# Slot tiles of a top-1 expert layer: rows turned by DMA transposes, the expert's middle feature-major, the gate at the output, three tiles in a runtime branch

## The chip, the cores and the metric

The kernel runs on one core of a Trainium2 chip. The time is the device time of one execution in microseconds; the time given for a kernel is the median over its runs. A profiled execution has a time of its own, and the span of its trace lies inside that time.

## The reference

Attention over 8 batches, 12 heads, 448 positions and head size 64, with queries and keys normalised by their root mean square, gives a matrix x of 3584 tokens by 768 features. On it follows a feed-forward layer with a dense part and eight experts, of which each token takes one:

```python
h_dense = np.maximum(x @ w1_dense, 0.0)
y_dense = h_dense @ w2_dense
logits = x @ w_gate
expert_idx = np.argmax(logits, axis=1)
...
gate_w = probs[np.arange(N), expert_idx]
for e in range(E):
    mask = expert_idx == e
    h = np.maximum(x[mask] @ w1[e], 0.0)
    y_moe[mask] = gate_w[mask, None] * (h @ w2[e])
return (y_dense + y_moe).astype(np.float32)
```

Here w1 and w1_dense are 768 by 512, w2 and w2_dense 512 by 768. The inputs are the same random draw each time.

## The kernel before

The kernel has two stages. In the first, `period(g)` walks through the attention, two heads at a time per step, and along with it computes for finished batches the expert choice, the gate and the dense part's hidden layer `relu(x @ w1_dense)`. For each token it writes one record of 704 words to a table in DRAM, `rec`: 768 bf16 values of x, 512 bf16 values of the dense hidden layer, the gate as a float, and padding. All expert weights are loaded into one SBUF tile `we` during this stage.

The second stage begins at line 528. Tokens are sorted by expert into slots; 128 slots make a slot tile, and each slot tile belongs to one expert, so that an expert's last tile may be partly empty. For 3584 tokens and eight experts there are at most NTL = 3584/128 + 7 = 35 tiles, and the kernel runs all 35, whether they hold tokens or not: an empty slot reads the record of row 0 and has an output row out of bounds, which is not written. Lines 534 to 597 compute on VectorE, from the counts of each expert, the row of each slot (`row`), its output row (`dest`) and the expert of each tile (`tei`, int32).

For each tile t the steps are:

- `gather(t)`: an indirect DMA on the POOL queue brings 128 records to `xg`.
- `xtrans(t)`: ten TensorE transposes turn the x values (six blocks of 128 columns) and the dense hidden values (four) into PSUM; VectorE copies them to `xT` and `hdT` (lines 614 and 619).
- `gemm1(t)`: TensorE loads the expert's number from `tei` into a register. Six matmuls, with a block of `xT` as the stationary operand and 512 columns of the expert's first weight as the moving one, give 128 tokens by 512 hidden features. ScalarE applies relu and, as the scale, the gate (line 630).
- `htrans(t)`: four TensorE transposes turn this hidden tile; ScalarE copies it to `heT` (line 637).
- `gemm2(t)`: eight matmuls of 384 columns with the dense hidden values and eight with the expert's add up in one PSUM tile `yp`. VectorE copies one half to `ys`, then ScalarE the other (lines 655 and 656), and an indirect DMA on POOL scatters the rows to the output (line 657).

The order on TensorE and on POOL is written out by hand at the end (lines 666 to 684): after a start-up, iteration t issues `gather(t + 4)`, `gemm1(t + 1)`, `xtrans(t + 2)`, `gemm2(t)` and `htrans(t + 1)`. The last weight load is issued on POOL in iteration 0. VectorE and ScalarE are ordered by the framework. The SP queue has nothing to do in this stage. A matmul is issued as two instructions, a load of the stationary operand (PEld) and the multiplication with the moving one (PE). Where an operand lies in `we` at a place that depends on the expert's register, TensorE's sequencer computes the address with a register instruction ahead of it (FUSED_REGOPS in the trace).

Of the kernel before, what the change touches and what calls it, by code (L numbers as in the profile page):

```python
# [9 lines left out]
F32 = mybir.dt.float32  # L10
BF16 = mybir.dt.bfloat16
I32 = mybir.dt.int32
AF = mybir.ActivationFunctionType
ALU = mybir.AluOpType
# [4 lines left out]
def kernel(  # L19
# [14 lines left out]
    nc = tc.nc  # L34
    P = 128
    B, H, S, D = q.shape
    N = B * S
    Dm = H * D
    E = moe_w_gate.shape[1]
    F = moe_w1_dense.shape[1]  # L40
# [4 lines left out]
    KD = Dm // P  # L45
    FT = F // P
    HD = Dm // 2
    De = D + 1
    scale = 1.0 / (D ** 0.5)
    PE, DVE, ACT, POOL, SP = (mybir.EngineType.PE, mybir.EngineType.DVE,  # L50
                              mybir.EngineType.Activation, mybir.EngineType.Pool,
                              mybir.EngineType.SP)
# [5 lines left out]
    ident = const.tile([P, P], BF16)  # L58
# [13 lines left out]
    NTL = N // P + E - 1  # L72
# [3 lines left out]
    GO = XH + F // 2  # L76
    RC = GO + 64
# [18 lines left out]
    we = const.tile([P, E, 2, KD * F], BF16)  # L96
# [3 lines left out]
    def constants():  # L100
# [11 lines left out]
        for hh in range(2):  # L112
# [3 lines left out]
            for n in range(NC4):  # L116
# [7 lines left out]
    wjobs = [(wgb, moe_w_gate.rearrange("(ko p) e -> p ko e", p=P)),  # L124
             (wd1, moe_w1_dense.rearrange("(ko p) f -> p ko f", p=P)),
             (wd2, moe_w2_dense.rearrange("(fo p) d -> p fo d", p=P))]
# [6 lines left out]
    one = ctx.enter_context(tc.tile_pool(name="m_one", bufs=1))  # L133
    with tc.tile_pool(name="a_ld", bufs=2) as ld, \
# [3 lines left out]
        xin, sqs, ssqs, rs, xn, qkT, exs, xas, xTs, avs, trs, xps = [{} for _ in range(12)]  # L138
# [132 lines left out]
        def xtrans(g):  # L271
            b, gb = divmod(g, NPR // GP)
            if g + 4 >= NG:
                trs["x"] = wkp.tile([P, 1024], BF16, tag="wk", name="xt")
            ps = trs["x"][:, :GP * S].rearrange("p (i s) -> p i s", i=GP)
            for i in range(GP):
                for m in range(4):
                    nc.tensor.transpose(  # L278
                        ps[:, i, QC[m]:QC[m] + P],
                        xas[b][:, m, (gb * GP + i) * P:(gb * GP + i + 1) * P], ident)  # L280
            xps[g] = trs["x"][:, :GP * S]
# [102 lines left out]
        def period(g):  # L384
            b, gb = divmod(g, NB)
            more = g + 2 < NG, g + 3 < NG
            for i in range(J):
# [3 lines left out]
                if i == 0:  # L391
                    if g > 1:
                        xtrans(g - 2)
                    if more[0]:
                        normalise(g + 2, "k")
                        normalise(g + 2, "q")
                    if gb != 1:
                        fill(g, KD)
# [60 lines left out]
        def run(order):  # L459
            with tc.manual_schedule(engines=order):  # L460
# [43 lines left out]
                for g in range(NG):  # L504
                    period(g)

                xtrans(NG - 2)
                xturned(NG - 2)
                fill(NG, KD)
# [16 lines left out]
        run({PE, POOL, SP, DVE, ACT})  # L526

    with tc.tile_pool(name="m_sb", bufs=5) as sb, \
         tc.tile_pool(name="m_p1", bufs=3, space=bass.MemoryType.PSUM) as ps1, \
         tc.tile_pool(name="m_p2", bufs=2, space=bass.MemoryType.PSUM) as ps2, \  # L530
         tc.tile_pool(name="m_ph", bufs=1, space=bass.MemoryType.PSUM) as psh, \
         tc.tile_pool(name="m_py", bufs=1, space=bass.MemoryType.PSUM) as psy:

        cnt = counts[B % 2]
        cmp = one.tile([P, E, NM], F32, tag="w1")
# [6 lines left out]
        tsi = one.tile([P, E], F32)  # L542
# [13 lines left out]
        for c in (slice(0, NC4 // 2), slice(NC4 // 2, NC4)):  # L556
# [3 lines left out]
            for i in range(2):  # L560
                nc.vector.tensor_mul(val[:, i, :, c], tl[:, :, c],
                                     tok[:, i, c].unsqueeze(1).to_broadcast(shape))
        slp = ps2.tile([P, 2, NTL], F32, tag="he")
        for n in range(NC4):
            nc.tensor.matmul(slp, sel[:, n // 4, n % 4], val[:, :, :, n],
                             start=(n == 0), stop=(n == NC4 - 1))
        sl = one.tile([P, 2, NTL], F32)
        nc.vector.tensor_copy(sl, slp)
        t1 = one.tile([P, NTL], F32)
        nc.vector.scalar_tensor_tensor(t1, in0=sl[:, 0], scalar=float(D), in1=sl[:, 1],  # L570
                                       op0=ALU.mult, op1=ALU.add)
# [5 lines left out]
                                ts[:1].unsqueeze(1).to_broadcast([1, NTL, E]), ALU.is_ge)  # L577
        te = one.tile([1, NTL], F32)
        nc.vector.tensor_reduce(te, tcm, AX.X, ALU.add)
        tei = one.tile([1, NTL], I32)  # L580
        nc.vector.tensor_scalar(tei, te, 1.0, None, op0=ALU.subtract)

# [9 lines left out]
                                       op0=ALU.mult, op1=ALU.add)  # L592
        nc.vector.scalar_tensor_tensor(t2, in0=sl[:, 1], scalar=float(J), in1=t2,
                                       op0=ALU.mult, op1=ALU.add)
        dest = one.tile([P, NTL], I32)
        nc.vector.scalar_tensor_tensor(dest, in0=t2, scalar=float(S - J + 1), in1=emp,
                                       op0=ALU.subtract, op1=ALU.add)

        xgs, xTs, hdTs, hes, heTs, eregs, stores = {}, {}, {}, {}, {}, {}, []

        def gather(t):
            xg = sb.tile([P, RC], F32, tag="xg", name="xg")
            nc.gpsimd.indirect_dma_start(  # L603
                out=xg, out_offset=None, in_=rec,
                in_offset=bass.IndirectOffsetOnAxis(ap=row[:, t:t + 1], axis=0))
            xgs[t] = xg

        def xtrans(t):
            xb = xgs[t].bitcast(BF16)
            xp = ps1.tile([P, KD, P], BF16, tag="tr")  # L610
            for kk in range(KD):
                nc.tensor.transpose(xp[:, kk], xb[:, kk * P:(kk + 1) * P], ident)
            xTs[t] = sb.tile([P, KD, P], BF16, tag="xT", name="xT")
            nc.vector.tensor_copy(xTs[t], xp)  # L614
            hp = ps1.tile([P, FT, P], BF16, tag="tr")
            for i in range(FT):
                nc.tensor.transpose(hp[:, i], xb[:, Dm + i * P:Dm + (i + 1) * P], ident)
            hdTs[t] = sb.tile([P, FT, P], BF16, tag="hdT", name="hdT")
            nc.vector.tensor_copy(hdTs[t], hp)

        def gemm1(t):
            eregs[t] = nc.tensor.value_load(tei[:, t:t + 1], min_val=0, max_val=min(t, E - 1))
            he = ps2.tile([P, F], F32, tag="he")
            for kk in range(KD):
                nc.tensor.matmul(he, xTs[t][:, kk],  # L625
                                 we[:, bass.ds(eregs[t], 1), 0, kk * F:(kk + 1) * F]
                                 .rearrange("p o f -> p (o f)"),
                                 start=(kk == 0), stop=(kk == KD - 1))
            hes[t] = sb.tile([P, F], BF16, tag="hs", name="hs")
            nc.scalar.activation(hes[t], he, AF.Relu, scale=xgs[t][:, GO:GO + 1])  # L630

        def htrans(t):
            hp = psh.tile([P, FT, P], BF16, tag="hp")
            for i in range(FT):
                nc.tensor.transpose(hp[:, i], hes[t][:, i * P:(i + 1) * P], ident)  # L635
            heTs[t] = sb.tile([P, FT, P], BF16, tag="heT", name="heT")
            nc.scalar.copy(heTs[t], hp)  # L637

        def gemm2(t):

            yp = psy.tile([P, 2, 512], F32, tag="y")
            for i in range(FT):
                for dd in range(2):
                    nc.tensor.matmul(yp[:, dd, :HD], hdTs[t][:, i],  # L644
                                     wd2[:, i, dd * HD:(dd + 1) * HD],
                                     start=(i == 0), stop=False)
            for i in range(FT):
                for dd in range(2):
                    nc.tensor.matmul(yp[:, dd, :HD], heTs[t][:, i],  # L649
                                     we[:, bass.ds(eregs[t], 1), 1,  # L650
                                        i * Dm + dd * HD:i * Dm + (dd + 1) * HD]
                                     .rearrange("p o f -> p (o f)"),
                                     start=False, stop=(i == FT - 1))
            ys = sb.tile([P, 2, HD], F32, tag="ys")
            nc.vector.tensor_copy(ys[:, 0], yp[:, 0, :HD])  # L655
            nc.scalar.copy(ys[:, 1], yp[:, 1, :HD])  # L656
            i = nc.gpsimd.indirect_dma_start(  # L657
                out=out, out_offset=bass.IndirectOffsetOnAxis(ap=dest[:, t:t + 1], axis=0),
                in_=ys.rearrange("p a d -> p (a d)"), in_offset=None,
                bounds_check=N - 1, oob_is_err=False)  # L660

            for j in stores:
                tc.declare_no_dep(i.ins, j.ins, reason="each token has one slot")
            stores.append(i)

        with tc.manual_schedule(engines={PE, POOL}):
            for t in range(4):
                gather(t)
            for t in range(2):
                xtrans(t)  # L670
            gemm1(0)
            htrans(0)
            for t in range(NTL):
                if t + 4 < NTL:
                    gather(t + 4)
                if t == 0:
                    nc.gpsimd.dma_start(*wjobs[-1])
                if t + 1 < NTL:
                    gemm1(t + 1)
                if t + 2 < NTL:  # L680
                    xtrans(t + 2)
                gemm2(t)
                if t + 1 < NTL:
                    htrans(t + 1)


# [28 lines left out]
```

## Time and profile before

| | us |
|---|---|
| runs | 462.23, 461.86, 455.8 |
| median | 461.86 |
| profiled execution | 458.04 |
| span of its trace | 456.3 |

| engine | busy us | share of the span |
|---|---|---|
| PE (matmul) | 384.7 | 84% |
| PEld (weight load) | 239.3 | 52% |
| DVE | 255.7 | 56% |
| ACT | 238.8 | 52% |
| POOL | 240.6 | 53% |

The mean granted TensorE clock is 0.956. In the slot stage the first gather is issued at 277.24 us, the first matmul of `gemm1` starts at 284.01, and the last matmul of the kernel ends at 451.07.

Engines are PE (TensorE's matmuls), PEld (its weight loads), DVE (VectorE), ACT (ScalarE), POOL (GpSimd) and SP (SyncE); a name with q is the engine's sequencer or queue, so PEldq holds TensorE's register instructions. A row such as `L625 PE MATMUL he<-we,xT` stands for the instructions of line 625 that write tile `he` from `we` and `xT`. The page cuts the span into 40 slices and gives each engine's busy share in tenths; PEclk is the granted clock in tenths. Busy times of pipelined matmuls overlap, so that the distance between two starts says what a matmul costs in a stream, and its duration doesn't.

### The profile page before, as it was taken

How to read it: one execution, taken by the hardware profiler on the slowest of the kernel's cores; microseconds unless marked ns; L12 is line 12 of the kernel's file. 1: busy time of each engine (PE TensorE's matmuls, PEld its weight loads, DVE VectorE, ACT ScalarE, POOL GpSimd, SP SyncE). 2: the span in 40 equal slices, each digit the busy share in tenths (PEclk: the TensorE clock that was granted, in tenths of full speed). 3: DMA queues.
4: the chain of work that ended last, by engine and by line, in shares of the span. 5: the costliest groups of instructions: out<-in, count | busy, mean ns of one | idle time of the engine just before them, and what ended most of it. 6: DMA issues, size and time to landing. Idle time of an engine off the chain costs nothing.

```text
span 456.3 us, 13950 instructions
## 1 busy us (share of the span) xinstructions
PE 384.7 (84%) x5628; PEld 239.3 (52%) x5628; DVE 255.7 (56%) x744; ACT 238.8 (52%) x394; POOL 240.6 (53%) x275
## 2 busy tenths in 40 slices
PE   0557777988969889798897954899999999999994
PEld 0234554555645556455564633466666666666662
DVE  2565679788897888978875553233232333323230
ACT  2735677785876868768687210333242333334241
POOL 2385887596775877759651105134444353444422
PEclk9999989998998999989999995999999999999998
DMA  8579395977979689796669984553544545354420
GB/s 212 185 112 244 100 249 144 225 153 222 228 229 213 135 241 225 230 213 139 157 100 200 178 194 133 110 172 121 174 129 147 165 137 167 127 171 154 161 95 1
DMA packets 49759, 76.32 MB, mean 167 GB/s; under 512 B 8541, under 2 KB 45661, under 8 KB 49696
## 3 DMA queue, kind: packets, MB, share of 16 engines
q0 software_dynamic: 24544, 43.31, 43.7%
q1 hardware_dynamic: 24832, 32.12, 22.4%
q8 instruction: 46, 0.75, 0.7%
q14 instruction: 17, 0.14, 0.1%
q10 hardware_dynamic: 320, 0.00, 0.0%
HBM read 73.98 MB, written 23.86 MB: 214 GB/s over the span
## 4 chain that ended last, share of the span: by engine, by line
issue 32%; DVE 21%; PE 21%; POOL 16%; ACT 4%; DMA 4%; POOLq 1%; ACTq 0%; DVEq 0%
DVE ssq L192 8%; PE ff L365 8%; POOL xg L603 7%; PE av L259 5%; DVE xa L268 4%; PE sc L241 3%; PE xt L278 3%; POOL out_dram L657 3%; POOL sq L187 3%; DVE y L227 2%; DVE y L229 2%; DMA records<-hd 2%; ACT we L244 2%; DVE y L211 2%; DMA gk<-in_g_k_dram 2%
## 5 line engine op out<-in xcount | busy, mean ns | idle before, releaser
L244 ACT ACTIVATE we<-sc 128x896 bf16<-128x896 f32 x168 | 147.0, 917 | 46.3 <-PE sc L241 45.7
L657 POOL DMA_INDIRECT out_dram<-ys,dest x35 | 35.3, 1010 | 95.2 <-ACT ys L656 90.5
L241 PE MATMUL sc<-y 64*64 64x448 bf16 x672 | 69.9, 408 | 7.9 <-ACT we L244 5.2
L637 ACT COPY heT<-hp 128x512 bf16<-128x512 bf16 x35 | 20.5, 585 | 91.7 <-PE hp L635 91.7
L259 PE MATMUL av<-va,we 64*128 64x65 bf16 x2688 | 63.9, 198 | 4.4 <-issue 3.5
L259 PEld LDWEIGHTS <-we 64*128 64x128 bf16 x2688 | 51.4, 99 | 26.4 <-issue 23.2
L211 POOL TENSOR_TENSOR y<-xk,r 128x448 bf16<-128x448 f32 x46 | 42.1, 937 | 41.7 <-ACT r L205 41.7
L192 DVE TENSOR_REDUCE ssq<-sq 128x7 f32<-128x448 f32 x96 | 55.4, 611 | 12.0 <-POOL sq L187 7.9
L655 DVE COPY ys<-yp 128x384 f32<-128x384 f32 x35 | 19.5, 558 | 72.5 <-issue 55.7
L365 PE MATMUL ff<-wd,xT 128*128 128x512 bf16 x192 | 52.1, 413 | 8.3 <-DVE xa L268 5.6
L625 PE MATMUL he<-we,xT 128*128 (+1 forms) x210 | 52.3, 386 | 0.5 <-issue 0.5
L644 PE MATMUL yp<-wd,hdT 128*128 128x384 bf16 x280 | 51.2, 326 | 1.1 <-ACT ys L656 1.1
L649 PE MATMUL yp<-we,heT 128*128 (+1 forms) x280 | 51.2, 326 | 0.0
L603 POOL DMA_INDIRECT xg<-records,row x35 | 34.5, 986 | 30.4 <-DVE t L591 20.0
L187 POOL TENSOR_TENSOR sq<-xk 128x448 f32<-128x448 f32 x44 | 40.7, 938 | 16.8 <-DVE ssq L192 16.7
L614 DVE COPY xT<-xp 128x768 bf16<-128x768 bf16 x35 | 19.5, 558 | 51.0 <-PE he L625 35.0
L219 PE MATMUL tr<-ident,y 128*128 128x128 bf16 x336 | 26.9, 237 | 20.0 <-DVE y L211 15.0
L268 DVE TENSOR_TENSOR xa<-av,inv 128x256 bf16<-128x256 f32 x96 | 40.8, 425 | 3.3
L187 POOL TENSOR_TENSOR sq<-xq 128x448 f32<-128x448 f32 x44 | 40.1, 932 | 0.0
L630 ACT ACTIVATE hs<-he,xg 128x512 bf16<-128x512 f32 x35 | 24.0, 687 | 27.8 <-PE he L625 18.1
L241 PEld LDWEIGHTS <-y 64*64 64x64 bf16 x672 | 20.5, 107 | 32.9 <-issue 22.9
L649 PEld LDWEIGHTS <-heT 128*128 128x128 bf16 x280 | 27.4, 98 | 18.1
(105 smaller groups left out, 475.6 us busy)
## 6 DMA issues: line engine op xcount, KB each, us to landing
we<-in_moe_w_dram POOLq DMA_DIRECT2D x16, 768.0 KB
xq<-in_q_dram SPq DMA_DIRECT2D x24, 448.0 KB, 4.8
xk<-in_k_dram SPq DMA_DIRECT2D x24, 448.0 KB, 5.7
xv<-in_v_dram POOLq DMA_DIRECT2D x11, 448.0 KB
records<-xa SPq DMA_DIRECT2D x8, 576.0 KB, 9.2
records<-hd SPq DMA_DIRECT2D x24, 128.0 KB, 3.9
wd<-in_moe_w_dense_dram POOLq DMA_DIRECT2D x2, 768.0 KB
records<-xa SPq DMA_DIRECT2D x8, 96.0 KB, 9.0
```

What stands on the lines that cost most here:

```text
L187: nc.gpsimd.tensor_mul(sqs[name, g, hh], x, x)
L192: nc.vector.tensor_reduce(ssqs[g][:, "qk".index(name), hh], sqs[name, g, hh].rearrange("p (j d) -> p j d", d=D), AX.X, ALU.add)
L211: eng.tensor_mul(y[:, :, hh], xin[name, g][:, hh].rearrange("p (j d) -> p j d", d=D), rs[name, g][:, hh].unsqueeze(2).to_broadcast([P, J, D]))
L241: nc.tensor.matmul(ps[r * D:(r + 1) * D, hh, :S], kT[rows, r, j], qT[rows, r].rearrange("p j s -> p (j s)"), start=True, stop=True)
L244: nc.scalar.activation(x, ps[:, :, :S], AF.Exp, scale=scale)
L259: nc.tensor.matmul(avs[hh, r][:, m], exs[g, j][rows, hh, QC[m]:QC[m] + P], va[rows, hh, j, :De], start=(j == 0), stop=(j == J - 1))
L268: nc.vector.tensor_mul(xas[b][:, :, h * D:(h + 1) * D], avs[hh, r][:, :, :D], inv.to_broadcast([P, 4, D]))
L365: nc.tensor.matmul(ff[0], xTs[b][:, kk, QC[m]:QC[m] + P], wd1[:, kk], start=(kk == 0), stop=(kk == KD - 1))
L603: nc.gpsimd.indirect_dma_start(out=xg, out_offset=None, in_=rec, in_offset=bass.IndirectOffsetOnAxis(ap=row[:, t:t + 1], axis=0))
L625: nc.tensor.matmul(he, xTs[t][:, kk], we[:, bass.ds(eregs[t], 1), 0, kk * F:(kk + 1) * F] .rearrange("p o f -> p (o f)"), start=(kk == 0), ...
L644: nc.tensor.matmul(yp[:, dd, :HD], hdTs[t][:, i], wd2[:, i, dd * HD:(dd + 1) * HD], start=(i == 0), stop=False)
L649: nc.tensor.matmul(yp[:, dd, :HD], heTs[t][:, i], we[:, bass.ds(eregs[t], 1), 1, i * Dm + dd * HD:i * Dm + (dd + 1) * HD] .rearrange("p o ...
```

## The change

The slot stage is rewritten; the first stage and the computation of `row`, `dest` and `tei` stay.

- `xtrans` goes. In its place `turn(t)` issues one DMA transpose on the SP queue that turns all 1280 bf16 columns of `xg` into `xT` with ten blocks of 128.
- `gemm1` computes the hidden tile feature-major: the stationary operand is a 128 x 128 block of the expert's first weight, the moving one a block of `xT`, so that 24 matmuls of 128 columns take the place of six of 512, and `htrans` goes too. ScalarE applies relu alone.
- `gemm2` keeps its sixteen matmuls, but the dense and the expert's part go to two PSUM tiles. ScalarE copies the dense part to `ds`; VectorE multiplies the expert's part by the gate and adds `ds`.
- The loop becomes the function `slots(t0, t1)`. It runs for the first NT1 = 32 tiles; after them every engine loads the number of tiles in use (`tct`), and the last three run in a branch that is taken only if that number is over 32.
- Buffers: `xg` has seven in place of five; the PSUM pools are two banks for the hidden tile and three double banks for the outputs.

```diff
-        def xtrans(t):
-            xb = xgs[t].bitcast(BF16)
-            xp = ps1.tile([P, KD, P], BF16, tag="tr")
-            for kk in range(KD):
-                nc.tensor.transpose(xp[:, kk], xb[:, kk * P:(kk + 1) * P], ident)
...
+        def turn(t):
+
+            xTs[t] = sb.tile([P, KD + FT, P], BF16, tag="xT", name="xT")
+            nc.sync.dma_start_transpose(xTs[t], xgs[t].bitcast(BF16)[:, :2 * GO])
+
+        def gemm1(t):
+
+            eregs[t] = nc.tensor.value_load(tei[:, t:t + 1], min_val=0, max_val=min(t, E - 1))
+            he = psh.tile([P, FT, P], F32, tag="he")
             for i in range(FT):
...
+                for kk in range(KD):
+                    c = kk * F + i * P
+                    nc.tensor.matmul(he[:, i],
+                                     we[:, bass.ds(eregs[t], 1), 0, c:c + P]
+                                     .rearrange("p o f -> p (o f)"), xTs[t][:, kk],
+                                     start=(kk == 0), stop=(kk == KD - 1))
+            hTs[t] = sb.tile([P, FT, P], BF16, tag="hT", name="hT")
+            nc.scalar.activation(hTs[t], he, AF.Relu)
...
-            yp = psy.tile([P, 2, 512], F32, tag="y")
+            yd = psy.tile([P, 2, 512], F32, tag="y", name="yd")
             for i in range(FT):
                 for dd in range(2):
-                    nc.tensor.matmul(yp[:, dd, :HD], hdTs[t][:, i],
+                    nc.tensor.matmul(yd[:, dd, :HD], xTs[t][:, KD + i],
                                      wd2[:, i, dd * HD:(dd + 1) * HD],
-                                     start=(i == 0), stop=False)
+                                     start=(i == 0), stop=(i == FT - 1))
+            ds = sb.tile([P, 2, HD], F32, tag="ds")
+            nc.scalar.copy(ds, yd[:, :, :HD])
+            ye = psy.tile([P, 2, 512], F32, tag="y", name="ye")
...
-            nc.vector.tensor_copy(ys[:, 0], yp[:, 0, :HD])
-            nc.scalar.copy(ys[:, 1], yp[:, 1, :HD])
+            nc.vector.scalar_tensor_tensor(ys, in0=ye[:, :, :HD], scalar=xgs[t][:, GO:GO + 1],
+                                           in1=ds, op0=ALU.mult, op1=ALU.add)
...
+        def slots(t0, t1, weights=None):
+            ahead = 4
+            for t in range(t0, min(t0 + ahead, t1)):
                 gather(t)
+                turn(t)
+            gemm1(t0)
+            for t in range(t0, t1):
+                if t + ahead < t1:
+                    gather(t + ahead)
+                    turn(t + ahead)
+                if t == t0 and weights:
+                    nc.gpsimd.dma_start(*weights)
+                if t + 1 < t1:
+                    gemm1(t + 1)
                 gemm2(t)
...
+        NT1 = N // P + E // 2
+        with tc.manual_schedule(engines={PE, POOL, SP}):
+            slots(0, NT1, wjobs[-1])
+        used = nc.values_load(tct, min_val=1, max_val=NTL)
+        with tc.If(used > NT1):
+            with tc.manual_schedule(engines={PE, POOL, SP}):
+                slots(NT1, NTL)
```

More of the change, by code (lines that the diff above doesn't have):

```diff
@@ L528 @@
     with tc.tile_pool(name="m_sb", bufs=5) as sb, \
[L529 to L532, printed above, removed]
+         tc.tile_pool(name="m_ph", bufs=2, space=bass.MemoryType.PSUM) as psh, \
+         tc.tile_pool(name="m_py", bufs=3, space=bass.MemoryType.PSUM) as psy:
         cnt = counts[B % 2]
@@ L562 @@
                                      tok[:, i, c].unsqueeze(1).to_broadcast(shape))
-        slp = ps2.tile([P, 2, NTL], F32, tag="he")
+        slp = psh.tile([P, 2, NTL], F32, tag="he")
         for n in range(NC4):
@@ L579 @@
         nc.vector.tensor_reduce(te, tcm, AX.X, ALU.add)
+        tct = one.tile([1, 1], I32)
+        nc.vector.tensor_copy(tct, tsi[:1, E - 1:])
         tei = one.tile([1, NTL], I32)
@@ L597 @@
                                        op0=ALU.subtract, op1=ALU.add)
-        xgs, xTs, hdTs, hes, heTs, eregs, stores = {}, {}, {}, {}, {}, {}, []
+        xgs, gts, xTs, hTs, eregs, stores = {}, {}, {}, {}, {}, []
         def gather(t):
-            xg = sb.tile([P, RC], F32, tag="xg", name="xg")
+            xg = sb.tile([P, RC], F32, tag="xg", name="xg", bufs=7)
             nc.gpsimd.indirect_dma_start(
@@ L606, in gather @@
             xgs[t] = xg
-        def xtrans(t):
-            xb = xgs[t].bitcast(BF16)
-            xp = ps1.tile([P, KD, P], BF16, tag="tr")
-            for kk in range(KD):
[L612 to L619, printed above, removed]
+        def turn(t):
+            xTs[t] = sb.tile([P, KD + FT, P], BF16, tag="xT", name="xT")
+            nc.sync.dma_start_transpose(xTs[t], xgs[t].bitcast(BF16)[:, :2 * GO])
@@ L621, in gemm1 @@
         def gemm1(t):
             eregs[t] = nc.tensor.value_load(tei[:, t:t + 1], min_val=0, max_val=min(t, E - 1))
[L623 to L629, printed above, removed]
@@ L630, in gemm1 @@
-            nc.scalar.activation(hes[t], he, AF.Relu, scale=xgs[t][:, GO:GO + 1])
-        def htrans(t):
-            hp = psh.tile([P, FT, P], BF16, tag="hp")
-            for i in range(FT):
-                nc.tensor.transpose(hp[:, i], hes[t][:, i * P:(i + 1) * P], ident)
-            heTs[t] = sb.tile([P, FT, P], BF16, tag="heT", name="heT")
-            nc.scalar.copy(heTs[t], hp)
+            he = psh.tile([P, FT, P], F32, tag="he")
+            for i in range(FT):
+                for kk in range(KD):
[4 more added lines that the diff above has]
+                                     start=(kk == 0), stop=(kk == KD - 1))
@@ L647, in gemm2 @@
+            ds = sb.tile([P, 2, HD], F32, tag="ds")
+            nc.scalar.copy(ds, yd[:, :, :HD])
+            ye = psy.tile([P, 2, 512], F32, tag="y", name="ye")
             for i in range(FT):
                 for dd in range(2):
-                    nc.tensor.matmul(yp[:, dd, :HD], heTs[t][:, i],
+                    nc.tensor.matmul(ye[:, dd, :HD], hTs[t][:, i],
                                      we[:, bass.ds(eregs[t], 1), 1,
@@ L652, in gemm2 @@
                                      .rearrange("p o f -> p (o f)"),
-                                     start=False, stop=(i == FT - 1))
+                                     start=(i == 0), stop=(i == FT - 1))
             ys = sb.tile([P, 2, HD], F32, tag="ys")
-            nc.vector.tensor_copy(ys[:, 0], yp[:, 0, :HD])
-            nc.scalar.copy(ys[:, 1], yp[:, 1, :HD])
+            nc.vector.scalar_tensor_tensor(ys, in0=ye[:, :, :HD], scalar=xgs[t][:, GO:GO + 1],
+                                           in1=ds, op0=ALU.mult, op1=ALU.add)
             i = nc.gpsimd.indirect_dma_start(
@@ L664, in gemm2 @@
             stores.append(i)
-        with tc.manual_schedule(engines={PE, POOL}):
-            for t in range(4):
+        def slots(t0, t1, weights=None):
+            ahead = 4
+            for t in range(t0, min(t0 + ahead, t1)):
                 gather(t)
[L669 to L678, printed above, removed]
+                turn(t)
[7 more added lines that the diff above has]
+                if t + 1 < t1:
                     gemm1(t + 1)
-                if t + 2 < NTL:
-                    xtrans(t + 2)
                 gemm2(t)
-                if t + 1 < NTL:
-                    htrans(t + 1)
+        NT1 = N // P + E // 2
[5 more added lines that the diff above has]
+                slots(NT1, NTL)
 _INS = ['q', 'k', 'v', 'g_q', 'g_k', 'moe_w_gate', 'moe_w1_dense', 'moe_w2_dense', 'moe_w1', 'moe_w2']
```

## The prediction

> **What bounds the kernel now.** I read the page's slices first, then the busy time of each engine in the even part of the slot stage, the TensorE groups there, and last the starts of TensorE's own register instructions within one tile.
>
> ```profile
> PE   0557777988969889798897954899999999999994
> PEclk9999989998998999989999995999999999999998
> DMA  8579395977979689796669984553544545354420
> ```
>
> Attention ends in slice 24; the rest, 284 to 451 us, is the slot stage that the change rewrites. There PE is full at the full clock, and DMA is half used. The even part by engine (length in us; busy us and instructions of PE, PEld, DVE, ACT, POOL; granted clock, DMA share, GB/s), then its TensorE groups (busy us, mean ns | idle before):
>
> ```profile
> 297.30:441.00 143.70, 143.70 (x1110) 90.21 (x1109) 44.86 (x93) 51.26 (x93) 59.16 (x60) 1.00 0.46 148
> ```
> ```profile
> L625 PE MATMUL he<-we,xT 128*128 x186 | 45.2, 379 | 0.0
> L644 PE MATMUL yp<-wd,hdT 128*128 128x384 bf16 x246 | 45.0, 326 | 0.0
> L649 PE MATMUL yp<-we,heT 128*128 x244 | 44.7, 326 | 0.0
> L612 PE MATMUL xp<-ident,xg 128*128 128x128 bf16 x186 | 15.4, 219 | 0.0
> L635 PE MATMUL hp<-ident,hs 128*128 128x128 bf16 x124 | 12.0, 219 | 0.0
> L617 PE MATMUL hp<-ident,xg 128*128 128x128 bf16 x124 | 12.0, 219 | 0.0
> ```
>
> No idle time in any group: the array is the bound. A matmul's duration includes its pipeline; starts are the price. Read one by one they lie 216 ns apart for 512 columns (L625), 162.5 for 384 (L644, L649), 56 for the 128-column transposes. A tile is 6 x 216 + 10 x 56 + 16 x 162.5 + 4 x 56 = 4.68 us, the period seen; 35 tiles are 163.8 us.
>
> Beside the array runs TensorE's sequencer (PEldq): before each matmul whose weights lie at a register's address it computes that address. One tile's share, with the expert number's load behind it:
>
> ```profile
> L649 PEldq FUSED_REGOPS  x8: 55/55/55, 383.4 to 384.4; - x8
> ```
> ```profile
> L622 PEldq TENSOR_LOAD <-tei x1: 298/298/298, 384.5 to 384.5; - x1
> L622 PEldq FUSED_REGOPS  x1: 151/151/151, 384.9 to 384.9; - x1
> L622 PEldq SEQ_ASSERT  x1: 18/18/18, 385.1 to 385.1; - x1
> ```
>
> The eight starts lie 133 ns apart (median of both lines' gaps), though the array takes their matmuls every 162.5: this is the sequencer's pace ahead of the array. TENSOR_LOAD also starts 133 ns after the last of them, although L635's four transposes stand between in program order: matmuls at fixed addresses take no sequencer time that shows. From TENSOR_LOAD to L625's first register instruction are 0.684 us. So before, the sequencer needs 14 x 0.133 + 0.684 = 2.55 us of 4.68, hidden.
>
> **The change, part by part.** Transposes: 14 x 56 = 0.78 us of array per tile go, with L614, L619 and L637. Expert GEMM 1 becomes 24 matmuls of 128 columns; by the transposes' spacing 24 x 56 = 1.34 us, for 6 x 216 = 1.30. GEMM 2 keeps 16 x 162.5 = 2.60. The array falls to 3.94 us per tile.
>
> [...]
>
> But all 24 matmuls now have their stationary operand at a register's address. The trace has that only on the moving side. If a weight load so addressed is paced like the matmul so addressed, the sequencer needs (24 + 8) x 0.133 + 0.684 = 4.94 us per tile, over the array's 3.94, and sets the pace. From below: 55 ns, the register instruction alone, gives 24 x 0.055 + 1.75 = 3.07, under the array, so 3.94 holds. From above: if load and matmul both carry the register, each pays another 133 - 55 = 78 ns: 24 x 0.211 + 1.75 = 6.81. I take 133, the nearest row: same instruction, same operands, one register user behind it.
>
> ACT per tile: relu at L630's 0.69 and the copy of 768 columns, two of L656's 0.485 at most: 1.66 us. DVE: multiply-add over 768, twice L655's 0.56 at most: 1.12. POOL: 0.99 + 1.01. All hide under 4.94; the copy releases yd early and three output buffers turn, so no PSUM wait arises.
>
> SP's queue gets 32 DMA transposes of 320 KB, with nothing else in it. None is in the trace. Engine time: by bytes at the SP queue's mean (32.12 MB in 22.4% of 456.3 us, 314 GB/s) 1.04 us; as 1,280 packets of 256 B at 22.8 ns (that size on that queue) over 16 engines 1.82; at that queue's mean of 65.9 ns per packet 5.27. I take 1.82. Gather and store use 0.46 x 4.68 = 2.15, so 3.97 of 4.94: hidden, cover about 1 us. Latency: a gather waits on POOL behind the store of the tile five earlier; from the end of that tile's GEMM 2 run 1.2 (output) + 1.0 + 1.0 (POOL) + 3.3 (landing, by the first gather: issued 277.24 to 278.29, used 281.56) + T, with three periods, 14.8 us, until its GEMM 1. T may be 8.3 us. SP's own issues land like this:
>
> ```profile
> records<-hd SPq DMA_DIRECT2D x24, 128.0 KB, 3.9
> records<-xa SPq DMA_DIRECT2D x8, 576.0 KB, 9.2
> ```
>
> I take 4.5; the ends are 2.9 (its quickest store) and 9.2, where 0.3 us per tile would show.
>
> [...]
>
> Last three tiles: the reference's draw gives the experts 409, 528, 432, 430, 448, 366, 478 and 493 tokens: 4+5+4+4+4+3+4+4 = 32 tiles, so the branch is not taken. The profile agrees: the last stores move almost nothing.
>
> ```profile
> 446.00:451.00 5.00, 3.89 (x26) 2.22 (x24) 0.56 (x1) 0.97 (x2) 0.98 (x1) 1.00 0.01 0
> ```
>
> The price is a register load per engine and a branch: 0.68 us by L622's rows, if the final store hides nothing; from nothing (it hides all) to 4. I take 2.
>
> Sum, from the first GEMM 1 to the last matmul. Before: 284.01 to 451.07, 167.1 us. After: 0.6 until the queue takes tile 1's load, 3.88 for its GEMM 1, 30 x 4.94 = 148.2, and 2.6 for the last GEMM 2: 155.3, so -11.8. The start: T of 4.5 in place of 2.45 (281.56 to 284.01): +2. The end: +2; the multiply-add replaces two copies of 0.56 and 0.48 in a row. Together -7.8: 450.2 against the profiled execution's 458.04, which lies 3.8 under the median of 461.86; 454 against that. Its own range: a load paced at 118 to 140 ns (31 x 24 x -15 to +7 ns: -11 to +5) and 3 for both ends: 440 to 462.
>
> **The rivals.** (a) The array paces: the load is cheap for the sequencer. 32 x 3.94 and 1.5 of start and end are 127.6: -39.5 + 4 = 426. For it: fixed-address loads cost the sequencer nothing. Against: an address in a register goes through it in every row.
> (b) Slower: both instructions of a pair pay for the register. 0.6 + 5.75 + 30 x 6.81 + 2.6 = 213.3, +46.2 + 4 = 512. It decides from 5.3 us per tile, 147 ns per pair. For it: the matmul names the same operand. Against: in L649 the plain load adds nothing.
> (c) Slower: DMA. At 5.27 + 2.15 = 7.4 us per tile the stage takes 237, +70 + 4 = 536; it binds from 2.8 us of engine time per transpose, or T over 8.3. Against it: 256-byte packets at 22.8 ns.
> (d) The change saves nothing by skipping, if rounding made a 33rd tile: the nearest expert is 16 tokens from a boundary, so I leave it out.
>
> **How the numbers follow.** About 2% is what a measurement of this kernel can tell from no change: 452.6 and 471.1. The sequencer's case has 0.56; its range lies across 452.6, so 0.28 of it counts as faster, 0.26 as the same, 0.02 as slower. (a) 0.14, (b) 0.12, (c) 0.12, and 0.06 for a dear branch or a clock that falls while GEMM 1 runs thin, of which 0.04 slower. Faster 0.42, same 0.28, slower 0.30. The range reaches from (a) to just over (b), 424 to 515, and leaves out most of (c); the likeliest case's own is 440 to 462.
>
> **What would show it.** Right: GEMM 1's matmuls start 133 ns apart with PE idle by issue, register instructions x24 per tile at that spacing, a period near 4.9, DMA under 0.9. Starts at 56 to 60 and a period of 3.9 are (a); 200 and more are (b); PE waiting for the transposes' tile is (c). The prediction is wrong if the period is off 4.94 by over 0.3, or the start or the branch costs over 5.

## The result and the profile after

The changed kernel takes 541.61 us (median of 4 runs, 540.64 to 544.97) against 460.38 for the kernel before on the same occasions: a ratio of 1.1795 (the two medians alone give 1.176) with a 95% interval of 1.1688 to 1.1902. It is slower by about 18%. Some executions of one kernel take some per cent longer at a lower granted clock (in the first experiment 455.6 and 463.8 us at 0.911 and 0.898, beside 450.7 and 447.5 at 0.942 and 0.939); where a kernel below had such runs, the time given first is that of its other runs. The profiled execution of the changed kernel took 541.67 us with a span of 540.0, which is 83.7 us more than the span before.

The page's slices of the changed kernel; the slot stage now reaches from slice 22 to the end:

```profile
PE   0666879898988888998725999999999999999992
PEclk9998889999899989998956878788989988989887
DMA  8496965987978896679959255475555446655411
```

PE still reads nearly full, the granted clock is no longer full, and DMA has stayed at half. So the busy share hides what happened; a stretch of the stage and the lines of GEMM 1 (now L620) show it. First the stretch (length in us; busy us and instructions of PE, PEld, DVE, ACT, POOL; granted clock, DMA share, GB/s):

```profile
300.00:500.00 200.00, 192.48 (x1073) 101.82 (x1071) 27.49 (x27) 37.12 (x53) 54.12 (x54) 0.89 0.54 135
```

All of L620's instructions, with what ended PE's and PEld's idle time before them:

```profile
L620 PEldq FUSED_REGOPS  x1488: 51/55/60, 287.8 to 522.8; - x186
L620 PEld LDWEIGHTS <-we x768: 95/96/152, 286.4 to 522.8; 128*128 x186, 128*128 128x128 bf16 x6
L620 PE MATMUL he<-xT,we x768: 216/217/311, 286.4 to 522.9; 128*128 128x128 bf16 x192
...
  issue: 31.7, 75
  DMA xg<-records,row: 13.6, 1
  DMA xT<-xg: 3.5, 1
```

There are 1488 register instructions, that is 48 for each of the 31 tiles whose expert is not known when the program is built: two per pair, where GEMM 1 before had 204 in all, one per matmul. After the first two tiles neither PE nor PEld waits for a DMA transpose; what ends their idle time is "issue" (31.7 us in 75 entries), and the starts within one tile in the middle put that down to TensorE's own sequencer:

```profile
L620 PEldq FUSED_REGOPS  x48: 51/55/60, 404.9 to 410.4; - x48
L620 PEld LDWEIGHTS <-we x24: 95/96/98, 406.9 to 410.4; 128*128 x24
L620 PE MATMUL he<-xT,we x24: 216/218/219, 407.1 to 410.5; 128*128 128x128 bf16 x24
```

The 48 stand 113 ns apart (median), 5.5 us from first to last. The first twelve pairs, whose register instructions had run ahead while GEMM 2 was busy, start 56 ns apart; from there on each pair waits for its two register instructions and the starts lie 227 ns apart. The load and the matmul each start 104 ns after a register instruction of their own; of all 744 pairs this holds, to within 6 ns, for 7 loads in 10 and 7 matmuls in 10. The rows name `we` twice: the 24 loads read it, and the 24 matmuls are listed with it beside `xT`; 48 is their sum. That the sequencer computes the same address for both, once for each instruction that names the weight, is my reading of these counts; whether the matmul needs its own, no run here tried.

From one load of the expert's number to the next lie 7.53 us (mean of 25 tiles): 0.72 to the first register instruction of GEMM 1, 5.55 from the first to the last of its 48, 0.18 to the first of GEMM 2's eight, 0.97 from the first to the last of these, and 0.12 to the next load. Where the 83.7 us of span went:

| stretch | before | after | difference |
|---|---|---|---|
| start of the span to the first gather | 277.2 | 274.7 | -2.5 |
| first gather to the first GEMM 1 | 6.8 | 11.7 | +5.0 |
| first GEMM 1 to the start of the last matmul | 166.7 | 242.7 | +76.0 |
| start of the last matmul to the end | 5.6 | 10.8 | +5.2 |

The first row is the unchanged stage and differs like this from run to run (275.9 us in the first experiment).

### The profile page after: what moved, and what is told of

It is laid out like the page before. It is cut to its first block, busy times and chain, and to the rows that moved or that the text cites. A ratio compares the mean times of both kernels' runs of the same rounds, so it can differ in the third digit from the quotient of the medians.

```text
span 540.0 us, 15140 instructions
## 1 busy us (share of the span) xinstructions
PE 448.8 (83%) x5648; PEld 258.4 (48%) x5648; DVE 237.7 (44%) x672; ACT 225.7 (42%) x353; POOL 234.9 (44%) x269
## 4 chain that ended last, share of the span: by engine, by line
issue 36%; DVE 19%; PE 18%; POOL 12%; DMA 9%; ACT 3%; POOLq 0%; ACTq 0%; DVEq 0%
DMA xg<-records,row 7%; PE ff L365 7%; DVE ssq L192 7%; POOL xg L603 5%; PE av L259 4%; DVE xa L268 3%; PE sc L241 3%; PE xt L278 3%; POOL sq L187 2%; DVE y L227 2%; DVE y L229 2%; POOL out_dram L648 2%; ACT we L244 2%; DVE y L211 1%; DMA gk<-in_g_k_dram 1%
## 5 line engine op out<-in xcount | busy, mean ns | idle before, releaser
L620 PE MATMUL he<-xT,we 128*128 128x128 bf16 x768 | 131.6, 224 | 25.7 <-DMA xg<-records,row 13.6
L646 DVE SCALAR_TENSOR_TENSOR ys<-ye,xg,ds 128x768 f32<-128x768 f32 x32 | 32.6, 1018 | 223.0 <-PE ye L640 186.1
L648 POOL DMA_INDIRECT out_dram<-ys,dest x32 | 32.3, 1010 | 183.9 <-DVE ys L646 181.2
L620 PEld LDWEIGHTS <-we 128*128 (+1 forms) x768 | 67.2, 98 | 89.9 <-issue 30.1
L625 ACT ACTIVATE hT<-he 128x512 bf16<-128x512 f32 x32 | 19.1, 598 | 177.7 <-PE he L620 169.3
L632 PE MATMUL yd<-wd,xT 128*128 128x384 bf16 x256 | 62.6, 402 | 0.0
L640 PE MATMUL ye<-we,hT 128*128 (+1 forms) x256 | 52.9, 355 | 0.0
L603 POOL DMA_INDIRECT xg<-records,row x32 | 31.7, 990 | 27.6 <-DVE t L591 18.1
L636 ACT COPY ds<-yd 128x768 f32<-128x768 f32 x32 | 25.6, 799 | 37.3 <-PE yd L632 37.3
L640 PEld LDWEIGHTS <-hT 128*128 128x128 bf16 x256 | 27.7, 108 | 22.5 <-issue 9.0
L632 PEld LDWEIGHTS <-xT 128*128 128x128 bf16 x256 | 28.0, 115 | 21.3 <-issue 12.8
```

The costliest lines, as they stand in the source:

```text
L603: nc.gpsimd.indirect_dma_start(out=xg, out_offset=None, in_=rec, in_offset=bass.IndirectOffsetOnAxis(ap=row[:, t:t + 1], axis=0))
L620: nc.tensor.matmul(he[:, i], we[:, bass.ds(eregs[t], 1), 0, c:c + P] .rearrange("p o f -> p (o f)"), xTs[t][:, kk], start=(kk == 0), stop= ...
L632: nc.tensor.matmul(yd[:, dd, :HD], xTs[t][:, KD + i], wd2[:, i, dd * HD:(dd + 1) * HD], start=(i == 0), stop=(i == FT - 1))
L640: nc.tensor.matmul(ye[:, dd, :HD], hTs[t][:, i], we[:, bass.ds(eregs[t], 1), 1, i * Dm + dd * HD:i * Dm + (dd + 1) * HD] .rearrange("p o f ...
```

## The experiments

The theory: the sequencer's register instructions, two per pair because, as I read it, both the load and the matmul name the expert's weight, set the pace. The rival: the DMA transposes do, in engine time or in landing.

**GEMM 1 token-major again**. The rest is as in the changed kernel, but two PSUM tiles for the transposes take the place of one of the three double banks for the outputs:

```diff
-            for i in range(FT):
-                for kk in range(KD):
...
+            for kk in range(KD):
+                nc.tensor.matmul(he, xTs[t][:, kk],
+                                 we[:, bass.ds(eregs[t], 1), 0, kk * F:(kk + 1) * F]
+                                 .rearrange("p o f -> p (o f)"),
+                                 start=(kk == 0), stop=(kk == KD - 1))
...
+        def htrans(t):
...
+            hTs[t] = sb.tile([P, FT, P], BF16, tag="hT", name="hT")
+            nc.scalar.copy(hTs[t], hp)
```

> The changed kernel with GEMM 1 put back token-major (x as the stationary operand, 512 columns of the expert's weight as the moving one) and its four transposes on TensorE; DMA transposes, gate at the output and branch stay. Theory (register instructions pace the stage: 48 per tile in GEMM 1 at 113 ns, because load and matmul of a pair each compute the weight's address): register instructions fall to 14 per tile, the array takes over with 6 x 216 + 16 x 162.5 + 4 x 56 = 4.12 us per tile against 7.45 in the changed kernel, so 32 x 3.3 = 107 us less: about 435. Rival (the DMA transposes, in engine time or in landing, pace the stage): the period stays over 5 us and the time over 460, up to 540 unchanged.

It took 449.1 us (mean of 450.74 and 447.5; all four runs reach from 447.5 to 463.8), 92 less than the changed kernel; from the first GEMM 1 to the last matmul 150.4 for 242.7. The theory holds for the 76 us, but the time is 14 over the 435 it gave: the mean period is 4.60 us, not 4.12. About half of the tiles keep the 4.12; the others take up to 6.9. The stretch of this kernel and two of its waits (us in total, times, longest) name the next bound:

```profile
297.30:420.00 122.70, 112.30 (x701) 64.66 (x700) 27.33 (x27) 53.27 (x81) 51.98 (x52) 1.00 0.92 214
```
```profile
PEld L619 <- DMA xT<-xg: 11.1, 9, 2.7
PE he L619 <- DMA xT<-xg: 10.2, 7, 2.6
```

The DMA engines are busy to 0.92, and GEMM 1 waits for the transposed tile.

**A fixed address in GEMM 1.** The tile, the sizes and the order stay; every tile takes expert 0's first weight:

```diff
-                                     we[:, bass.ds(eregs[t], 1), 0, c:c + P]
-                                     .rearrange("p o f -> p (o f)"), xTs[t][:, kk],
+                                     we[:, 0, 0, c:c + P], xTs[t][:, kk],
```

> The changed kernel, but GEMM 1 takes every tile's weight from expert 0 at a fixed address; which expert's first weight a tile uses is left out. The matmuls, their sizes and their number stay, only the register instructions of GEMM 1 go. Theory: the pace is the array's 24 x 56 + 16 x 162.5 = 3.94 us per tile, 32 x 3.5 = 112 us less: about 430; GEMM 1's matmuls start 56 ns apart. If the way from gather over DMA transpose to GEMM 1 binds next, 4.5 us per tile: 447. Rival (weight loads of 128 columns, the transposes or the half clock in every other tile set the pace): 520 or more.

447.5 us (one run), at the second number given: a mean period of 4.58. L620 has no register instruction left, its matmuls start 56 ns apart, and what GEMM 1 now waits for is the transpose:

```profile
L620 PE MATMUL he<-xT,we x768: 216/219/314, 286.4 to 429.8; 128*128 128x128 bf16 x192
...
  issue: 30.8, 17
  DMA xT<-xg: 18.3, 16
  DMA xg<-records,row: 14.2, 1
```
```profile
297.30:420.00 122.70, 109.94 (x1092) 79.33 (x1090) 28.51 (x28) 37.38 (x54) 55.13 (x55) 1.00 0.98 222
```

Of the issue time here, 14.4 us lie before the first tile, and 14 of the other 16 entries are loads held up beside a matmul that waits for the transpose. So 94 us go with the addresses alone, the 24 loads of 128 columns per tile do not set the pace, and the full clock comes back (1.00 for 0.89). The expectation named latency for its period of 4.5; the record points to engine time. By the packet records of the stretch from 300 to 420 us a transpose's 1,280 packets of 256 B take 28.1 ns each here (22.8 in the changed kernel), a gather's 64 take 324, a store's 64 take 279: 2.25 + 1.30 + 1.12 = 4.67 us of sixteen engines per tile, the period within 2%, at a DMA share of 0.98.

**TensorE transposes in place of the DMA transposes**, feature-major kept, PSUM divided as in the first experiment:

```diff
-            nc.sync.dma_start_transpose(xTs[t], xgs[t].bitcast(BF16)[:, :2 * GO])
...
+            for k0, n in ((0, KD), (KD, FT)):
+                xp = pst.tile([P, n, P], BF16, tag="tr", name="tr")
+                for kk in range(n):
+                    nc.tensor.transpose(xp[:, kk], xb[:, (k0 + kk) * P:(k0 + kk + 1) * P], ident)
+                nc.vector.tensor_copy(xTs[t][:, k0:k0 + n], xp)
```

> The changed kernel with ten TensorE transposes per tile and their two VectorE copies in place of the DMA transpose; feature-major GEMM 1, gate and branch stay. Theory: the array gets 0.56 us more per tile, the sequencer's 7.45 us stays the pace: 535 to 541, a few us less because the first GEMM 1 need not wait 7 us for a DMA transpose beside the weight loads. Rival (DMA transposes pace the stage): the array's 4.5 us per tile, 450.

540.4 us (one run), mean period 7.55. The DMA share falls to 0.29 and the time stays, which rules the rival out for the changed kernel:

```profile
300.00:500.00 200.00, 193.23 (x1333) 115.20 (x1331) 50.62 (x79) 37.08 (x53) 52.97 (x53) 0.91 0.29 92
```

From the first gather to the first GEMM 1 are 7.5 us here, 11.7 with the DMA transpose.

**No branch**: the lines from the load of the tile count on are taken out.

> The changed kernel with the register loads of the tile count and the branch taken out: tiles 32 to 34 are left out for good, which for this draw hold no tokens. From the last matmul to the end of the span the changed kernel has 10.7 us, the one before 5.2. Theory (the branch costs the difference): 536, the tail back at 5 to 6 us. Rival (the tail is the last store landing with data): 541, the tail stays over 9.

541.46 us (ratio to before 1.1744, interval 1.1642 to 1.1845): no difference from the changed kernel that can be measured, and the end takes 9.7 us instead of 10.8. The expectation of 536 was wrong: about 1 us of the end is the branch. What is long there is a DRAIN, one of three such instructions with which GpSimd ends the program (shortest, median and longest in ns; the kernel before, then the changed one):

```profile
L710 POOLq DRAIN  x3: 46/103/2822, 452.3 to 456.1; - x3
```
```profile
L707 POOLq DRAIN  x3: 46/109/7410, 531.7 to 539.7; - x3
```

The longest is 7.42 us without the branch. Below, "the DRAIN" is this longest one.

**One register user per pair**: the kernel before, each 512-column matmul cut into four.

```diff
-                nc.tensor.matmul(he, xTs[t][:, kk],
-                                 we[:, bass.ds(eregs[t], 1), 0, kk * F:(kk + 1) * F]
+                for i in range(FT):
+                    c = kk * F + i * P
+                    nc.tensor.matmul(he[:, i * P:(i + 1) * P], xTs[t][:, kk],
+                                     we[:, bass.ds(eregs[t], 1), 0, c:c + P]
...
```

> The kernel before, with each of the six 512-column matmuls of GEMM 1 cut into four of 128 columns; x stays the stationary operand, so of each pair only the matmul has a register's address, the load a fixed one. 24 + 8 register instructions per tile. Theory (a pair costs the sequencer 133 ns for one instruction with a register's address and 227 for two): sequencer 32 x 0.133 + 0.684 = 4.94 us per tile, just over the array's 10 x 56 + 24 x 56 + 16 x 162.5 + 4 x 56 = 4.73, so 35 x 0.26 = 9 us more than before: about 471, with 32 register instructions per tile 133 ns apart. Rival (small matmuls with computed addresses cost about 227 ns whichever operand carries the register): 24 x 0.227 + 1.75 = 7.2 us per tile, 35 x 2.5 = 88 more: 550.

487.1 us (a second run, the one traced, 495.8): over the theory's 471, far under the rival's 550. In the trace, 7.1 us of the excess over the kernel before lie in the unchanged first stage; from the first GEMM 1 to the last matmul it takes 197.3 us for 166.7, 31 more where the theory had 9 and the rival 88. One tile:

```profile
L627 PEldq FUSED_REGOPS  x24: 51/55/55, 384.6 to 387.7; - x24
L627 PEld LDWEIGHTS <-xT x24: 95/98/98, 385.8 to 387.7; 128*128 128x128 bf16 x24
L627 PE MATMUL he<-we,xT x24: 216/219/219, 385.9 to 387.8; 128*128 x24
```

One register instruction per pair, 133 ns apart (median), as the prediction had priced it; with two it is 227. But the period is 5.53 us and not 4.94: from the load of the expert's number to the first register instruction are 0.7 to 1.2 us instead of 0.68, the step from one group to the next takes 0.2, and gaps of up to 0.29 stand within the groups. The prediction had taken its prices from a tile in which the sequencer was ahead of the array; what lengthens them in this stream is open.

**The branch alone**, on the kernel before (32 tiles, then the test and the last three):

```diff
-            for t in range(NTL):
...
+        with tc.manual_schedule(engines={PE, POOL}):
+            slots(0, NT1, wjobs[-1])
+        used = nc.values_load(tct, min_val=1, max_val=NTL)
+        with tc.If(used > NT1):
+            with tc.manual_schedule(engines={PE, POOL}):
+                slots(NT1, NTL)
```

> The kernel before with the branch alone: 32 tiles, then the register loads of the tile count and the branch with the last three. Theory: three periods of 4.68 us less, 14.0; but the last store now carries 128 rows, and GpSimd's last DRAIN took 7.41 us in every run whose last tile holds tokens and 2.82 in the one before, where it holds none: 4.6 more. Together 9.4 less: 453. Rival (the empty tiles cost less than a full period, or the branch has a price of its own): 458 or more.

451.86 us (median of 4), ratio 0.978 (0.971 to 0.9849): in the trace 14.2 us less from the first GEMM 1 to the last matmul, 4.2 more at the end. The period stays 4.68.

**The x blocks alone by DMA** (e7_half_dma), from the third tile on, added to that; GEMM 1 stays token-major and the four dense hidden blocks stay on TensorE:

```diff
+        def turn(t):
+            xTs[t] = sb.tile([P, KD, P], BF16, tag="xT", name="xT")
+            nc.sync.dma_start_transpose(xTs[t], xgs[t].bitcast(BF16)[:, :Dm])
...
+            if t < 2:
                 xp = ps1.tile([P, KD, P], BF16, tag="tr")
```

> The kernel before with the branch, and with the six x blocks of each tile from the third on turned by a DMA transpose; the first two tiles' x blocks and all dense hidden blocks stay on TensorE, GEMM 1 stays token-major, the gate stays in the relu. Theory (with register instructions few, the larger of array and DMA paces the stage): array 6 x 216 + 16 x 162.5 + 8 x 56 = 4.34 us; DMA 1.23 + 1.10 for gather and store and 768 packets x 28 ns / 16 = 1.34 for the transpose, 3.67; so 32 x 4.34 = 139 for 35 x 4.68 = 163.8, less 4.6 at the end: 20 us under before, about 442. Rival (DMA transposes beside gathers delay GEMM 1 anyway, as at the start of the changed kernel, where they landed after 7 to 12 us): 453 or more, no better than the branch alone.

442.48 us (median of 6, 439.81 to 445.62), ratio 0.9586 (0.9536 to 0.9636): this version beats both kernels. The 442 of the sum is met, in part by luck: its terms made 20 us, and the traces show 14 (19.4 less from the first GEMM 1 to the last matmul, 1.1 more at the start, 4.2 more at the end); most of the rest is that the traced run of the kernel before, 458.04, lies 5 us under the median of the runs beside this one, 462.92. The stretch of the branch alone and of this version:

```profile
297.30:420.00 122.70, 122.70 (x950) 77.09 (x948) 38.45 (x80) 43.63 (x79) 53.02 (x53) 1.00 0.45 150
```
```profile
297.30:420.00 122.70, 121.00 (x832) 72.26 (x831) 27.10 (x55) 45.67 (x83) 54.08 (x54) 1.00 0.79 200
```

DMA has room at 0.79 and PE is nearly full; the mean period is 4.43 for the 4.34 expected and the 4.68 before.

**An empty scatter** (e8_empty_last), to see what sets the DRAIN, added to the last version (it reads any tile and writes no row):

```diff
+        i = nc.gpsimd.indirect_dma_start(
+            out=out, out_offset=bass.IndirectOffsetOnAxis(ap=none, axis=0),
+            in_=wd2.rearrange("p f d -> p (f d)").bitcast(F32)[:, :Dm], in_offset=None,
+            bounds_check=N - 1, oob_is_err=False)
```

> The kernel of e7_half_dma with one more scatter at the very end whose 128 rows are all out of bounds, so that it writes nothing. Theory: GpSimd's last DRAIN is 7.4 us when the scatter queued last carries rows and 2.8 when it carries none, as in the kernel before; then the end costs 1.3 us for one more scatter and wins 4.6: about 439 beside 442.5, with a DRAIN near 2.8. Rival: the DRAIN waits for all real rows that were scattered before it, then it stays at 6 to 7.4 us: 442 to 444.

The framework's scheduler put it at 46 us, where nothing held it. The DRAIN was 3.67 us all the same, with a last scatter of 128 rows, and the time, 437.8 and 440.6 us (all six runs reach to 449.4, ratio 0.9662, 0.9593 to 0.9731), is no gain that can be told from the version without. Two more followed, one with the scatter truly last (it reads the last output tile) and one with two early:

> As e8_empty_last, with the empty scatter truly last on POOL (it reads the last output tile). In e8 the scheduler had put it at 46 us, and GpSimd's last DRAIN was 3.67 us all the same, with a last scatter of 128 rows. Theory (what the scatter queued last carries sets the DRAIN): near 2.8 here. Second theory (the number of scatters queued in the whole program sets it, not what they carry): 3.7 as in e8, which has as many. Rival (it waits for all real rows): over 6.

> As e8_empty_last, with two empty scatters at the early place. Theory (what the last scatter carries): the last scatter carries rows, the DRAIN stays at 3.7 to 7.4 as it was with the same last scatter in e7 and e8, no statement between them. [...] Rival (run to run scatter): any of the two values.

They gave a DRAIN of 8.24 and 3.68 us (445.3 and 450.4 us for the kernels, one run each). Neither what the last scatter carries nor the number of scatters alone sets the DRAIN: the same number, 33, stands beside 3.67 and 8.24. Short (2.8 to 3.7) are the four programs in which a scatter without rows came before the last one, as the empty tiles do in the kernel before; long (7.4 to 8.2) the other eight. Why stays open.

## Why the prediction was wrong

The forecast was 454 us with a range of 424 to 515; 541.6 were measured. The step that failed is the price of a pair in GEMM 1: "I take 133, the nearest row: same instruction, same operands, one register user behind it." There are two users. The rows before could not show it, since there the expert's weight was the moving operand, which only the matmul reads. As the stationary operand it is named by the load and by the matmul, and the trace has a register instruction for each: 48 per tile, 227 ns per pair in place of 133, a period of 7.53 us in place of 4.94. This is rival (b), to which I gave 0.12. The reason against it, that in L649 the plain load adds nothing, is true of the loads at a fixed address there (133 ns per pair) and says nothing of the second user.

Point by point:

- What bounds the kernel before: right. Cutting three tiles took 14.2 us off the stage, three periods of 4.68 being 14.0, and six transposes less on the array shortened the period to 4.43.
- The array at 56 ns per pair: right, shown in the stretches where the sequencer had run ahead, and by the fixed address, with which GEMM 1's matmuls start 56 ns apart.
- The sequencer as the new bound, with PE idle by issue: right in kind, wrong in size. Even one user gave 5.53 us per tile in a stream and not 4.94, so the likeliest case was probably undersized too; by that period, an estimate since it comes from another kernel, 32 x 5.53 = 177 us would have been slower than before.
- Rival (b) in size: 512 forecast, 541.6 measured. Between the traces the difference is 33.5 us larger than in its sum: 30 periods of 7.53 for 6.81 are 22 (half of it the pair, 227 ns for 211, the other half the sequencer's other gaps), about 8 are the first two tiles, of which the second waits 3.5 for its transposed tile, 3 each the start and the end, and 2.5 less the unchanged stage. Against the medians it is 30, since the traced run of the kernel before lies 3.8 under its median.
- The DMA transposes: 1.82 us of engine time was right in the changed kernel (22.8 ns per packet from 300 to 420 us; 180 GB/s for 320 KB). Rival (a) left DMA out, although the 3.97 us summed for it were already over 3.94: with the fixed address, the sequencer out of the way, a transpose's packets took longer (28.1 ns), transposes, gathers and stores made 4.5 to 4.7 us of engine time per tile, and neither 3.94 nor 4.12 was reached as a mean (4.58 there, 4.60 with token-major GEMM 1).
- The landing T: 4.5 taken; from the issue of the transpose to GEMM 1 are 7.1 us for the first tile and 11.9 for the second, beside the last weight load (DMA share 1.05 from 284 to 297.3 us). In the even part it was nearer: after the first five tiles (7.5 to 13.6 us) the kernel with token-major GEMM 1 runs GEMM 1 within 4.3 to 8.8 us of the transpose's issue.
- The last three tiles: right. The end: 2 taken for the branch, 5.2 measured. The DRAIN alone is 4.6 longer, which no term of the sum held; the branch is about 1.

## What to carry to other kernels

Before a loop is given addresses from a register, count the users of each address: in these programs a stationary operand at a register's address had two, the load and the matmul (48 register instructions for 24 pairs), and the 24 small pairs, 1.34 us of the array at 56 ns each, did not hide the sequencer's 5.5. In the kernel before, the sequencer ran ahead of a busy array and showed its price only in the starts of its own instructions (133 ns apart beside matmuls 162.5 apart), and the price from there, an estimate of 4.94 us for a tile with one user per pair, fell short of the 5.53 seen in a stream. And keep the wide operand that the register picks as the moving one: six matmuls of 512 columns took six addresses here, 24 of 128 as weights took 48 (449.1 us for the first, 541.6 for the second).

## What the runs showed of the hardware

- A pair whose matmul has a register's address cost TensorE's sequencer 133 ns, in the kernel before and in one tile of the run with one register user; where load and matmul both have one, as in the changed kernel, 2 x 113 = 227. Pairs at fixed addresses cost it little or nothing that shows: in the kernel before, the next tile's load of the expert's number starts 133 ns after the last register instruction (0.16 us in the mean of 25 tiles), with four transposes between them.
- The granted clock was lower where GEMM 1 was thin: 0.89 from 300 to 500 us of the changed kernel, where about half of the pairs of the tile above start 227 ns apart, and 1.00 from 297.3 to 420 us with the fixed address, where they start 56 ns apart. That the one brings the other is not shown. In 14 of the changed kernel's 32 tiles GEMM 2's dense half takes 2.1 to 2.8 us, as in the first of these two consecutive tiles (start, length; the third line is the stretch around the first tile's, where the granted clock was 0.50):

```profile
403.10 2.76 PE L632 MATMUL yd<-wd,xT 128*128 128x384 bf16 x8
```
```profile
410.58 1.46 PE L632 MATMUL yd<-wd,xT 128*128 128x384 bf16 x8
```
```profile
402.50:405.80 3.30, 3.29 (x13) 1.66 (x13) 0.00 (x0) 0.60 (x1) 0.00 (x0) 0.50 0.56 169
```

It costs nothing that shows there, since the loads of the expert's number keep coming 7.35 to 7.8 us apart in both kinds of tile.

- GpSimd's longest DRAIN at the end took 2.8 to 3.7 us in four of the twelve kernels and 7.4 to 8.2 in the other eight, and no theory tried here explains which.
